# Float32 exponentials of the score tiles written back into their PSUM bank

## The chip, the cores and the metric

The kernel runs on one core of one Trainium2 chip. The metric is the device time of one execution in microseconds (us); lower is better. Engines are named as the profile names them: PE (TensorE, with PEld for its weight loads), DVE (VectorE), ACT (ScalarE), POOL (GpSimd) and SP (SyncE, which here issues most DMAs).

## What is computed

Three layers follow each other: causal attention with a decay bias (4 batches, 8 heads, 576 positions, head size 64), a mixture of 8 experts that gives each token to one expert, and a gated layer with a convolution of three taps. The change lies in the attention:

```
scores = scale * np.matmul(q, k.transpose(0, 1, 3, 2))
bias = -(cum[:, :, :, None] - cum[:, :, None, :])
scores = np.where(causal, -1000000000.0, scores + np.minimum(bias, 0.0))
scores = scores - np.max(scores, axis=-1, keepdims=True)
attn = np.exp(scores)
attn = attn / (np.sum(attn, axis=-1, keepdims=True) + 1e-09)
return np.matmul(attn, v).astype(np.float32)
```

## The kernel before

The attention works in 8 units of 4 heads each (two units to a batch). Matrix products run on float16 numbers in pairs: a float32 number is held as a high float16 part and a low one, the difference between the number and its high part.

A unit has 14 score tiles. A head has three tiles of 128 x 512 (`g` = 0, 1, 2), and every second head a fourth one of 128 x 64 columns (`g` = 3) for the last 64 positions of two heads. The program is one list of 112 steps, one score tile to a step, in a software pipeline that is written out by hand. In step t the loop at the end of `attention` issues, in this order:

- `rowmax` (L334, DVE): the row maxima of the piece of the step before, read from a PSUM tile `za`;
- `scores` of tile t (L438 and L441, PE): the products of `q` and `k` into a PSUM tile `z`;
- `piece` for a later unit (L331, PE): scores of the next unit into a PSUM tile `za`, from which its row maxima come, 14 pieces to a unit;
- `weights` of tile t-1 (L475 and L476, ACT): the exponential of `z`, once to float16 (`phi`) and once to float32 (`p`);
- `rest` of tile t-2 (L487, DVE): the difference `plo` = `p` - `phi`, a float16 tile;
- `values` (L503, PE) four steps behind, once for each head: the products of `phi` and `plo` with the values into a PSUM tile `o`; then `norm` and `xout` (L541 to L549, DVE) five and six steps behind.

One tile of each unit (third head, `g` = 0) is of another kind: its exponential stays one float32 tile `p0` (L471), and it has no difference.

When the last piece of a unit has been reduced, `max_cols` (L394 and L397, DVE) scales the maxima, `max_turn` (L407, PE) turns them and a DMA puts them into the operand of that unit's scores. POOL takes the low parts of `q` and `k` (L246, L247) and of `v` (L297 to L303), and those of the normed output (L560), all from SBUF into SBUF.

What keeps the engines in step are the buffers. There are three PSUM tiles `z` (pool `zps`), so `scores` of tile t need the bank of tile t-3. There are two PSUM tiles `za` (pool `aps`), so a piece needs the reduction of the piece two before it. `p` has three SBUF tiles (pool `pp`, named p32), `phi` and `plo` have eleven each. Each engine runs its own instructions in the order of the program, and waits on semaphores of the others.

After the attention (from about 263 us) come the routing of the tokens, a chain of small DVE instructions, the splitting of expert weights into two parts (L1034 on DVE), and the two other layers, in which PE is nearly always busy.

Of the kernel before, what the change touches and what calls it, by code (L numbers as in the profile page):

```python
# [9 lines left out]
F32 = mybir.dt.float32  # L10
F16 = mybir.dt.float16
# [27 lines left out]
def bc(ap, shape):  # L39
    return ap.to_broadcast(shape)  # L40


class Keep:
# [6 lines left out]
PAR = {'u1': {'sv': -6, 'pa': -10, 'pn': 4, 'mx': -3},  # L50
 'u2': {'at': (-24, -23, -20, -20, -19, -16), 'lv': -15, 'sv': -2, 'pa': -14, 'pn': 8, 'mx': -6},
 'u3': {'load': -37, 'loadq': 6, 'at': (-33, -28, -28, -27, -24, -22), 'sv': -1, 'pa': -19, 'pn': 14, 'mx': -5},
 'u': {'load': -48,
       'loadq': 8,
       'at': (-38, -34, -28, -31, -23, -23),
       'lv': -8,
       'sv': -4,
       'pa': -20,
# [56 lines left out]
def attention(tc, ctx, q, k, v, s, xd, rt, hook):  # L115
# [10 lines left out]
    def pool(n, b, on=ctx, **kw):  # L126
        return on.enter_context(tc.tile_pool(name=n, bufs=b, **kw))

    const, vp, natv = pool("const", 1), pool("vv", 2), pool("natv", 1)
    pp, p0p, php, wk, xp, xtp = pool("p32", 3), pool("p0", PAR["h"]["p0"]), pool("phl", PAR["h"]["ph"]), pool("wk", 2), pool("xs", 2), pool("xt", 1)  # L130
    zps, aps, ops, mps = (pool(n, b, space=PSUM) for n, b in (("zps", 3), ("aps", 2), ("ops", 2), ("mps", 1)))
    dram = pool("exd", 1, space=bass.MemoryType.DRAM)
    ex, ext = dram.tile([3, 2, B * H, 256], F16, name="ex"), dram.tile([3, B * H, 64], F16, name="ext")
# [292 lines left out]
    def mode(x):  # L426

        return PAR["m"][3 * x[1] + x[2]] if x[2] < 3 else "a"
# [36 lines left out]
    def weights(x):  # L465

        n = 64 if x[2] == 3 else 512
        z = st[x]
        if mode(x) == "f":
            p = st[x] = p0p.tile([128, 512], F32, name="p0")  # L470
            A.activation(p, z, AF.Exp, bias=lnes, scale=1.0 / SC)  # L471
            return
        p, hi, lo = pp.tile([128, 512], F32, name="p"), php.tile([128, 512], F16, name="phi"), php.tile([128, 512], F16, name="plo")
        if mode(x) != "p":
            A.activation(hi[:, 0:n], z[:, 0:n], AF.Exp, bias=lnes, scale=1.0 / SC)  # L475
        A.activation(p[:, 0:n], z[:, 0:n], AF.Exp, bias=lnes, scale=1.0 / SC)  # L476
        st[x] = p, hi, lo
# [137 lines left out]
    def second_a():  # L615
# [12 lines left out]
        z=lambda: Q.dma_start(xd[NT:NT + 128].rearrange("p (j c) -> p j c", c=256), bc(zero[:, None], [128, 4, 256])))  # L628
# [32 lines left out]
    for t in range(N + 9):  # L661
# [13 lines left out]
        if at(1):  # L675
            weights(at(1))
# [669 lines left out]
def attn_moe_moe2(tc, q, k, v, s, wg, wl, w1, w2, w_in, conv, w_out, out):  # L1346
    nc = tc.nc
    w_in, conv, w_out = (t.bitcast(I32) for t in (w_in, conv, w_out))
    with tc.manual_schedule(), ExitStack() as ctx:
# [40 lines left out]

        rt = Routing(tc, keep)
        attention(tc, c3, q, k, v, s, xd, rt, hook)
        c3.close()
        with ExitStack() as c4:
# [62 lines left out]
```

## Time and profile before

| what | us |
|---|---|
| median of 3 runs | 747.02 |
| lowest and highest run | 743.34 and 748.52 |
| the profiled execution, whole | 745.7 |
| its span, from first to last instruction | 743.5 |
| PE busy, share of the span | 85% |
| DVE busy, share of the span | 62% |
| ACT busy, share of the span | 52% |
| POOL busy, share of the span | 36% |

The profile is of one execution. Busy time is the union of an engine's instructions; register, semaphore and DMA-issuing instructions are not counted. Consecutive instructions of an engine overlap a little, so the next one can start before the row's duration is over. A wait is put down to what ended it last. The attention's score tiles lie between about 37 and 263 us; the steps of units 2 to 6 lie between 117 and 245 us.

### The profile page before, as it was taken

Reading aid. Unit: us, or ns where it says so; the run is one execution under the profiler, and the core shown is the slowest. Engines: PE = TensorE matmul, PEld = TensorE weight load, DVE = VectorE, ACT = ScalarE, POOL = GpSimd, SP = SyncE. Lnnn points to the kernel's source line nnn. Section 1 sums busy time; section 2 is a strip of 40 time slices with the busy share of each in tenths; the row PEclk is TensorE's granted clock in tenths of the full one; section 3 lists DMA queues with packets and bytes.
Section 4 is the critical chain, followed back from the end, with each engine's and each line's share of the span. In section 5 each row is a group of like instructions: output and inputs, shape, how many; then the busy total and the mean of one; then the engine's idle time right before and its main releaser. Section 6 shows DMA issues by size and latency. Waiting matters only on the chain.

```text
span 743.5 us, 15702 instructions
## 1 busy us (share of the span) xinstructions
PE 631.6 (85%) x5301; PEld 387.1 (52%) x5301; DVE 464.3 (62%) x838; ACT 383.3 (52%) x640; POOL 265.3 (36%) x367
## 2 busy tenths in 40 slices
PE   0449669988988934779999999999879999999997
PEld 0226547766766832334444444444347776666443
DVE  5527558987979787962587759675108994465000
ACT  4135647666767875543464737352109975455110
POOL 9316757655645247922243443433200000000000
PEclk9999879888989975998999999999989999999999
DMA  9977697878768895399999999966256400000111
GB/s 182 200 138 140 158 165 145 136 165 180 128 142 220 248 265 191 86 220 300 237 281 316 240 295 186 255 146 135 68 97 112 65 1 29 29 15 28 58 43 56
DMA packets 197278, 113.37 MB, mean 152 GB/s; under 512 B 147286, under 2 KB 173182, under 8 KB 197182
## 3 DMA queue, kind: packets, MB, share of 16 engines
q1 hardware_dynamic: 192574, 99.14, 58.5%
q0 software_dynamic: 4272, 12.93, 6.1%
q8 instruction: 48, 0.79, 0.4%
q14 instruction: 48, 0.39, 0.2%
q10 hardware_dynamic: 336, 0.11, 0.1%
HBM read 62.20 MB, written 15.31 MB: 104 GB/s over the span
## 4 chain that ended last, share of the span: by engine, by line
PE 49%; DMA 6%; DVE 1%; issue 0%; ACT 0%; another core or an unknown queue 0%; ACTq 0%; SPq 0%; DVEq 0%
PE hp L1270 13%; PE o L1318 13%; PE hp L1078 12%; PE yp L1078 11%; DMA yd<-ys,idx 4%; DMA ht<-hs 2%; PE xp L1108 1%; DVE r L1034 1%; DMA yt<-yd 0%; DVE hs L1124 0%; ACT xt L1109 0%; DVE ys L1138 0%; ACT ys L1137 0%; ACT s L1321 0%
## 5 line engine op out<-in xcount | busy, mean ns | idle before, releaser
L1078 PE MATMUL hp<-r,xt 128*128 x504 | 114.9, 385 | 8.4 <-ACT xt L1109 5.9
L1078 PE MATMUL yp<-r,ht 128*128 x504 | 112.2, 379 | 1.7 <-PEq L1186 1.1
L1270 PE MATMUL hp<-yt,wi 128*128 128x288 f16 x768 | 97.1, 289 | 2.9 <-DMA yt<-yd 2.9
L334 DVE TENSOR_REDUCE mx<-za 128x1 f32<-128x512 f32 (+4 forms) x113 | 67.7, 612 | 50.1 <-PE za L331 49.6
L1318 PE MATMUL o<-wo,g 128*128 128x512 f16 x432 | 94.5, 379 | 0.0
L487 DVE TENSOR_TENSOR plo<-p,phi 128x512 f16<-128x512 f32 (+1 forms) x104 | 85.1, 819 | 6.4 <-ACT p L476 6.2
L1270 PEld LDWEIGHTS <-wi 128*128 128x128 f16 x768 | 75.8, 99 | 24.5 <-DMA yt<-yd 3.4
L1078 PEld LDWEIGHTS <-xt 128*128 128x128 f16 x504 | 49.9, 99 | 69.5 <-ACT xt L1109 9.1
L475 ACT ACTIVATE phi<-z,lnes 128x512 f16<-128x512 f32 (+1 forms) x104 | 65.5, 629 | 39.3 <-PE z L441 39.2
L1078 PEld LDWEIGHTS <-ht 128*128 128x128 f16 x504 | 48.5, 98 | 57.4 <-issue 1.8
L331 PE MATMUL za<-k 70*128 70x256 f16 (+2 forms) x160 | 40.4, 338 | 41.3 <-DMA k<-k 33.6
L1034 DVE SCALAR_TENSOR_TENSOR r<-st,r 128x512 f32 (+3 forms) x76 | 69.3, 980 | 8.1 <-ACT r L1023 4.7
L438 PE MATMUL z<-k 71*128 71x256 f16 (+2 forms) x320 | 60.5, 311 | 12.3 <-ACT phi L475 6.7
L1139 POOL DMA_INDIRECT yd<-ys,idx x21 | 21.6, 1028 | 135.6 <-DVEq L1062 84.3
L1318 PEld LDWEIGHTS <-g 128*128 128x128 f16 x432 | 42.3, 98 | 49.5
L476 ACT ACTIVATE p<-z,lnes 128x512 f32<-128x512 f32 (+1 forms) x104 | 65.6, 631 | 1.2 <-DVE plo L487 1.1
L1023 ACT ACTIVATE r<-st 128x512 f32 (+3 forms) x84 | 57.0, 760 | 15.4 <-SPq L1071 12.5
L503 PEld LDWEIGHTS <-phi 128*128 128x128 f16 (+2 forms) x896 | 53.4, 108 | 4.8 <-issue 1.0
L503 PE MATMUL o<-vv,phi 128*128 128x65 f16 (+1 forms) x832 | 54.3, 203 | 0.0
L438 PEld LDWEIGHTS <-k 71*128 71x128 f16 x576 | 39.7, 106 | 22.7 <-issue 10.9
L503 PE MATMUL o<-vv,plo 128*128 128x65 f16 (+1 forms) x416 | 51.2, 200 | 0.0
L1287 DVE SCALAR_TENSOR_TENSOR c<-hb,cw,c 128x576 f32<-128x576 f32 x32 | 26.1, 816 | 36.7 <-ACT c L1281 36.7
(255 smaller groups left out, 1018.6 us busy)
## 6 DMA issues: line engine op xcount, KB each, us to landing
st<-in_moe_w_dram SPq DMA_DIRECT2D x8, 2048.0 KB
st<-in_moe_w_dram SPq DMA_DIRECT2D x24, 512.0 KB
out_dram<-s SPq DMA_DIRECT2D x18, 256.0 KB
st<-in_k_dram SPq DMA_DIRECT2D x16, 256.0 KB
st<-in_q_dram SPq DMA_DIRECT2D x16, 256.0 KB
k<-k SPq DMA_DIRECT2D x16, 256.0 KB
xd<-xh SPq DMA_DIRECT2D x16, 256.0 KB
k<-in_moe_w_dram SPq DMA_DIRECT2D x8, 512.0 KB
```

Of the source, the lines that this page charges most:

```text
L331: PE.matmul(out, lhsT=l, rhs=r, start=start, stop=stop, skip_group_check=True)
L334: return lambda: V.tensor_reduce(out, z.rearrange("p (e c) -> p e c", e=m), axis=AX.X, op=ALU.max)
L438: PE.matmul(out, lhsT=ks[i], rhs=qs[i], start=first and not i, stop=False, skip_group_check=True)
L475: A.activation(hi[:, 0:n], z[:, 0:n], AF.Exp, bias=lnes, scale=1.0 / SC)
L476: A.activation(p[:, 0:n], z[:, 0:n], AF.Exp, bias=lnes, scale=1.0 / SC)
L487: (V if md == "a" else G).tensor_tensor(lo[:, 0:n], p[:, 0:n], hi[:, 0:n], op=ALU.subtract)
L503: PE.matmul(out, lhsT=w, rhs=x, start=first, stop=last, skip_group_check=True)
L1023: i = self.nc.scalar.activation(hi, src, AF.Copy, scale=self.scale[w])
L1034: i = nc.vector.scalar_tensor_tensor(lo, in0=src, scalar=sc, in1=hi, op0=ALU.mult, op1=ALU.subtract)
L1078: i = self.nc.tensor.matmul(out, lhsT=lhsT, rhs=self.rings[w][:, c, k, bass.ds(s, 1), f], **kw)
L1270: PE.matmul(st[x][:, n, 0:HN], lhsT=wi[:, c, k, m], rhs=t[:, n, a + k], start=k + a + c == 0, stop=k == 3 and a == 4)
L1318: PE.matmul(o, lhsT=g[:, a, k, 128 * i:128 * i + 128], rhs=wo[:, c, k], start=j == 0, stop=j == 23)
```

## The change

For the tiles with two parts, the float32 exponential (L476) no longer goes to an SBUF tile `p` but back into the PSUM tile `z` from which it is read, and the difference (L487) reads it there. The SBUF pool p32 with its three tiles goes.

```
-    pp, p0p, php, wk, xp, xtp = pool("p32", 3), pool("p0", PAR["h"]["p0"]), pool("phl", PAR["h"]["ph"]), pool("wk", 2), pool("xs", 2), pool("xt", 1)
+    p0p, php, wk, xp, xtp = pool("p0", PAR["h"]["p0"]), pool("phl", PAR["h"]["ph"]), pool("wk", 2), pool("xs", 2), pool("xt", 1)
...
-        p, hi, lo = pp.tile([128, 512], F32, name="p"), php.tile([128, 512], F16, name="phi"), php.tile([128, 512], F16, name="plo")
+        p, hi, lo = z, php.tile([128, 512], F16, name="phi"), php.tile([128, 512], F16, name="plo")
         if mode(x) != "p":
             A.activation(hi[:, 0:n], z[:, 0:n], AF.Exp, bias=lnes, scale=1.0 / SC)
         A.activation(p[:, 0:n], z[:, 0:n], AF.Exp, bias=lnes, scale=1.0 / SC)
```

No instruction changes its place on any engine. What changes are the waits. On PE, the first tile of unit 2 stands in the program of before as follows (`k12` and `k2` are operands of that unit's scores, `k10` that of the piece for unit 3; a name in brackets is the engine or DMA queue whose semaphore is waited for):

```order
L438 LDWEIGHTS k12_143 [waits DMAHW7_49,DMAHW6_49]
L438 MATMUL z_1511<-k12_143 128x512 [waits Activation_49]
L438 LDWEIGHTS k2_619
L438 MATMUL z_1511<-k2_619 128x512
L441 LDWEIGHTS identm_135
L441 MATMUL z_1511<-trik_137,identm_135 128x128
L331 LDWEIGHTS k10_141
L331 MATMUL za_1515<-k10_141 128x256 [waits DVE_49]
```

And the same place now:

```order
L438 LDWEIGHTS k12_140 [waits DMAHW7_49,DMAHW6_49]
L438 MATMUL z_1483<-k12_140 128x512 [waits DVE_49]
L438 LDWEIGHTS k2_609
L438 MATMUL z_1483<-k2_609 128x512
L441 LDWEIGHTS identm_132
L441 MATMUL z_1483<-trik_134,identm_132 128x128
L331 LDWEIGHTS k10_138
L331 MATMUL za_1487<-k10_138 128x256 [waits PE_49]
```

The scores' first matmul waited for ACT (the exponentials of the tile three steps before) and now waits for DVE (the difference of that tile). The piece behind it waited for DVE (the reduction of the piece two before); that reduction stands in DVE's order ahead of the difference, so the earlier wait covers it.

## Rows read from the trace of the kernel before

**Rows 1.** The page: span; busy us, share of span, instructions per engine.

```profile
span 743.5 us, 15702 instructions
...
PE 631.6 (85%) x5301; PEld 387.1 (52%) x5301; DVE 464.3 (62%) x838; ACT 383.3 (52%) x640; POOL 265.3 (36%) x367
```

**Rows 2.** The chain that ended last: first piece (start us, us, what).

```profile
310.48 0.09 issue
```

**Rows 3.** Stretches: us; busy PE, PEld, DVE, ACT, POOL; clock, DMA share, GB/s.

```profile
45.00:117.00 72.00, 51.65 (x605) 38.74 (x606) 41.97 (x83) 38.05 (x70) 45.21 (x83) 0.88 0.77 149
117.00:245.00 128.00, 111.47 (x1728) 89.57 (x1727) 110.76 (x238) 86.73 (x160) 72.13 (x87) 0.88 0.76 162
245.00:263.00 18.00, 17.55 (x373) 15.45 (x371) 14.84 (x44) 16.32 (x33) 2.31 (x2) 1.00 0.93 275
263.00:335.00 72.00, 43.08 (x310) 22.75 (x308) 57.96 (x94) 39.59 (x58) 44.86 (x40) 0.80 0.74 186
```

**Rows 4.** The same stretches, line L487 (difference) alone: DVE busy us (x count).

```profile
45.00:117.00 72.00, 18.68 (x23) 0.88 0.77 149
117.00:245.00 128.00, 56.29 (x66) 0.88 0.76 162
245.00:263.00 18.00, 10.11 (x15) 1.00 0.93 275
```

**Rows 5.** Waits, 117 to 245 us: who, what for: us, times, longest.

```profile
DVE mx L334 <- PE za L331: 10.4, 16, 1.6
...
PE mt L407 <- DVE m L397: 6.8, 4, 2.0
PE za L331 <- DVE mx L334: 6.5, 9, 1.8
```

**Rows 6.** Of single lines: ns min/median/max, first and last start us, forms.

```profile
L487 DVE TENSOR_TENSOR plo<-p,phi x104: 194/684/2100, 46.9 to 262.3; 128x512 f16<-128x512 f32 x88, 128x64 f16<-128x64 f32 x16
...
L1124 DVE SCALAR_TENSOR_TENSOR hs<-hp,hs x42: 675/682/692, 309.1 to 517.7; 128x512 f16<-128x512 f32 x42
...
L547 DVE TENSOR_TENSOR x<-o,rc x32: 410/418/425, 70.9 to 264.7; 128x256 f32<-128x256 f32 x32
...
L476 ACT ACTIVATE p<-z,lnes x104: 303/679/780, 46.2 to 261.4; 128x512 f32<-128x512 f32 x88, 128x64 f32<-128x64 f32 x16
...
L1123 ACT ACTIVATE hs<-hp x42: 571/597/597, 301.7 to 515.3; 128x512 f16<-128x512 f32 x42
```

**Rows 7.** Timeline of DVE (start us, us, engine, line, operation), 189 to 210 us.

```profile
189.80 2.10 DVE L487 TENSOR_TENSOR plo<-p,phi 128x512 f16<-128x512 f32 x1
...
192.29 1.05 DVE L487 TENSOR_TENSOR plo<-p,phi 128x512 f16<-128x512 f32 x1
...
193.99 0.80 DVE L487 TENSOR_TENSOR plo<-p,phi 128x512 f16<-128x512 f32 x1
...
195.70 1.57 DVE L487 TENSOR_TENSOR plo<-p,phi 128x512 f16<-128x512 f32 x1
...
197.66 0.68 DVE L487 TENSOR_TENSOR plo<-p,phi 128x512 f16<-128x512 f32 x1
...
199.12 1.07 DVE L487 TENSOR_TENSOR plo<-p,phi 128x64 f16<-128x64 f32 x1
...
209.90 0.18 DVE L397 TENSOR_SCALAR m<-mx 128x18 f16<-128x18 f32 x1
```

**Rows 8.** Timeline of POOL, from the same stretch.

```profile
189.23 2.12 POOL L247 TENSOR_TENSOR st<-st,st 128x1024 f16<-128x1024 f32 x1
...
194.33 2.39 POOL L302 TENSOR_TENSOR vv<-nv,vv 128x1024 f16<-128x1024 f32 x1
```

**Rows 9.** Timeline of PE, from the same stretch.

```profile
196.62 0.62 PE L438 MATMUL z<-k 71*128 71x128 f16 x6
...
203.88 0.63 PE L438 MATMUL z<-k 71*128 71x128 f16 x6
...
210.14 0.28 PE L407 MATMUL mt<-id,m 128*18 128x128 f16 x1 [1.74 <-DVE m L397]
```

## Prediction

> **What bounds the kernel now.** I read the page first, then the chain that ended last, then the stretches of the attention, the line that the change touches, the waits, and at last one stretch step by step. The page shows no engine that is full over the whole span [rows 1]; an average over stages says little here. The chain is followed back only to 310.48 us [rows 2]; behind that point PE runs almost without a gap, and none of it is touched. What the change can move is when the attention ends, and so when the 72 us of routing and weight splitting begin, in which DVE is busy for 57.96 us with work in a fixed order [rows 3]. I take it that a microsecond saved in the attention is a microsecond saved at the end.
>
> Within the attention the stretch from 117 to 245 us (units 2 to 6) counts. Of its 128 us PE is busy for 111.47 and DVE for 110.76, ACT for 86.73, POOL for 72.13 [rows 3]. So two engines are near full, and each waits for the other: DVE for the pieces of PE 10.4 us, PE for reductions 6.5 us and for the scaled maxima 6.8 us [rows 5]. Neither is the only bound. In 45 to 117 us no engine is full (PE 51.65, DVE 41.97, POOL 45.21 of 72), and from 245 to 263 us PE is (17.55 of 18), with ACT behind it at 16.32 [rows 3].
>
> **Part one: the difference becomes shorter.** The 104 differences take 194 to 2100 ns, with a median of 684 ns [rows 6]. The long ones lie beside POOL: the one at 189.80 us took 2.10 us while POOL's subtraction ran from 189.23 for 2.12 us, and the one at 195.70 took 1.57 us and ended at 197.27, after POOL's that ran from 194.33 to 196.72 had ended; one at 197.66 took 0.68 us [rows 7, 8]. Both the difference and POOL's subtraction read two operands in SBUF. DVE instructions with one operand in PSUM and one in SBUF show no such spread: 42 at L1124, of the same shape, took 675 to 692 ns, and 32 at L547, within the attention and so beside the same work of POOL, 410 to 425 ns [rows 6]. The changed difference is of this kind. I take 0.684 us for a full one and 0.2 us for a narrow one.
>
> In 117 to 245 us the differences are busy for 56.29 us in 66 instructions [rows 4]: a unit has 11 full and 2 narrow ones, which makes 56 full and 10 narrow here. At the short durations they need 56 x 0.684 + 10 x 0.2 = 40.3 us. DVE is freed of 16.0 us. In the same way 45 to 117 us frees 18.68 - (19 x 0.684 + 4 x 0.2) = 4.9 us, and 245 to 263 us 10.11 - (12 x 0.684 + 3 x 0.2) = 1.3 us. The bounds of a full difference from PSUM are the 0.68 of L1124 and, if POOL still held it up, today's mean, at which nothing is freed; by form I take the nearest row, L1124.
>
> [...]
>
> **Part two: the bank is held longer, and PE gets a new wait.** There are three banks. Until now scores of tile t waited for the exponentials of tile t-3, now for its difference. An example: scores began at 196.62 us [rows 9], and the difference of the tile three before ran from 197.66 to 198.34 [rows 7], so they would have come 1.72 us later. Behind the waiting matmul stand the piece of the same step and, every three or four steps, the values of a head; DVE waits for the piece, ACT for the scores. The wait for the reduction of the piece two before [rows 5] (6.5 us) falls, as it is covered by the new one. In short: PE could run ahead of DVE by about a step more than it can now.
>
> What this costs next to part one I worked out by going through 189.8 to 210 us by hand, each instruction at its duration in the timeline and behind what it waits for, with differences of 0.68 and 0.2 us. The five long differences there (2.10, 1.05, 0.80, 1.57 and a narrow one of 1.07 [rows 7]) free 1.42 + 0.37 + 0.12 + 0.89 + 0.87 = 3.7 us. What comes of it: DVE now overtakes PE three times and waits some 0.65 us each, for the values and pieces of a head (PE does not reach the scores behind a head's values before about 203.35, at 203.88 now [rows 9]); PE waits for differences twice, 0.3 and 0.5 us, in the short steps without values; and the scaled maxima at 209.90 [rows 7], on which PE waits for 1.74 us before 210.14 [rows 9], come at about 208.5, 1.4 us earlier. So 1.4 of 3.7 us reach the end, a share of 0.38, the new wait included. For 117 to 245 us this makes 0.38 x 16.0 = 6.1 us.
>
> **Part three: the rest.** The exponential that now writes PSUM has no row. The bounds: 0.597 us, the shortest row of an activation of this shape (L1123), and 0.780, the longest of L476; today's median is 0.679 [rows 6]. I take 0.679. Even 0.10 more on 56 tiles is 5.7 us of ACT, which has 128 - 86.73 = 41 us to spare there. The exponential's own wait for the freeing of `p` goes with the pool; three `z` banks take the place of three `p` tiles. From 245 to 263 us there are no pieces, and each set of scores will follow a difference: one difference of 0.7 us is lost once, not per tile, since ACT is behind PE there; against it stands part of the 1.3 us freed. I count both at nothing, with bounds of -0.5 and +0.7. From 45 to 117 us I also count nothing: with PE and DVE idle for 20 and 30 of 72 us, the engines wait on loads and on POOL; its bounds are 0 and 0.38 x 4.9 = 1.9 us gained.
>
> **The sum.** The profiled execution took 745.7 us, 2.2 more than its span and 1.3 below the median of 747.0. 745.7 - 6.1 = 739.6; put to the median, 740.9, told as 741.0.
>
> **The rivals.**
> First, the coupling wins. Its place is the head: after each head's values DVE has nothing left, as PE can no longer have a piece in store. In the walk that was three waits of 0.65 us over three heads; if it is two such waits at each of the 20 heads of units 2 to 6, 20 x 1.3 = 26 us are lost and 16.0 freed, and the time is 747.0 + 10 = 757. It decides from 0.8 us of lost DVE time per head (16.0 / 20). For it speaks that DVE already waits 10.4 us for pieces [rows 5]; against it that the long differences are what makes DVE late in the first place.
> Second, the gain stays off the path: DVE is freed, but PE at 111.47 of 128 us, its slower clock (0.88 there [rows 3]) and the loads set the pace, and the two effects cancel: 746.5, from 745 to 748. For it speaks that PE is as full as DVE.
> Third, most of it arrives: the 13.3 us in which PE waits for DVE 6.5 + 6.8, [rows 5] go, and the pace is PE's: 747.0 - 13.3 = 733.7. Against it stands the walk, in which two thirds are lost.
> That the change does not do what it says, so that differences stay long beside POOL, would leave only the new wait: 1.72 us of lead lost once or twice in each of five units, 8.6 to 17 us, 756 to 764. L547 speaks against it; I count it with the first rival.
>
> **How the numbers follow.** The forecast has a chance of 0.48, the first rival 0.20, the second 0.20, the third 0.12. About 1% (7.5 us) is what a measurement of this kernel can tell from no change. The forecast's own range is 736 to 745. The range of 8 in 10 leaves out the far half of the first rival and the low end of the third: 732 to 754. Faster by over 1% (below 739.5): four tenths of the forecast's range, 0.20, and the third rival, 0.12, with a little over for its bounds: 0.33. Slower by over 1%: the first rival, 0.20. Within 1%: 0.47.
>
> **What would show it.** Right: every full difference at 0.68 to 0.70 us, also beside POOL, and L487 at some 63 us in all; DVE busy in the attention 20 us less; scores waiting for differences often, under 0.6 us each; the last difference 5 to 8 us earlier. Wrong: differences over 1 us; float32 exponentials of over 0.8 us; DVE's waits for pieces grown from 10 us to over 25; or an attention that ends early while the chain of the routing ends no earlier.

## The result

The changed kernel took 737.29 us (median of 4 runs, 735.95 to 738.79) beside 747.4 us for the kernel before on the same chip: a ratio of 0.9882, with a 95% interval of 0.9841 to 0.9924. Forecast were 741.0 us and a range of 732 to 754. Two more measurements, each beside its own runs of the kernel before, gave 0.987 (0.9818 to 0.9921) and 0.9972 (0.993 to 1.0014). So the gain lies between 0.3% and 1.3%, and the last measurement by itself cannot be told from no gain; the sections below come back to that. (The medians given here are of all runs; the ratios leave disturbed runs out, so the two can differ by some tenths of a per cent.)

The page of the changed kernel: span, and busy us of each engine, as [rows 1].

```profile
span 736.3 us, 15742 instructions
...
PE 625.4 (85%) x5301; PEld 383.7 (52%) x5301; DVE 443.8 (60%) x838; ACT 380.8 (52%) x640; POOL 251.2 (34%) x367
```

DVE lost 20.5 us and POOL 14.1: the two had held each other up, and both got shorter. POOL's subtraction of 128 x 1024 at L302 took 2052 to 2441 ns in the kernel before, with a median of 2367, and takes 2056 to 2073 now, with one of 2062. PE lost 6.2 us too, with the same 5301 matmuls, and no edit made a matmul shorter. Over the whole span it was granted a clock of 0.950, beside 0.940 before. These 6.2 us cannot be credited to the change: in a second trace of each kernel (again_before and third_after, below) PE is busy for 625.5 us in the kernel before and for 631.7 in the changed one. The stretches of the changed kernel (columns as in [rows 3]):

```profile
45.00:117.00 72.00, 51.45 (x580) 38.58 (x580) 38.91 (x85) 37.52 (x70) 42.33 (x85) 0.86 0.77 149
117.00:245.00 128.00, 111.92 (x1817) 90.32 (x1816) 98.20 (x252) 89.21 (x168) 62.24 (x87) 0.93 0.81 168
245.00:263.00 18.00, 15.57 (x335) 13.74 (x332) 12.20 (x38) 13.57 (x27) 1.15 (x1) 1.00 0.97 288
```

In the 128 us of the middle row DVE is busy for 98.20 us instead of 110.76. PE is busy as long as before (111.92 beside 111.47), but with 1817 matmul records instead of 1728, at a granted clock of 0.93 instead of 0.88. In this pair of traces more of the attention fits into the same stretch. The second trace of the kernel before shows that this is not steady: there the stretch has more records still, at 0.89.

```profile
117.00:245.00 128.00, 114.66 (x1839) 93.15 (x1839) 113.03 (x255) 91.14 (x170) 74.24 (x90) 0.89 0.80 168
```

The difference alone, in the same stretches (as [rows 4]), and its line with minimum, median and maximum in ns, with that of the exponential that now writes PSUM (as [rows 6]):

```profile
45.00:117.00 72.00, 14.26 (x23) 0.86 0.77 149
117.00:245.00 128.00, 41.79 (x69) 0.93 0.81 168
245.00:263.00 18.00, 7.18 (x12) 1.00 0.97 288
```

```profile
L487 DVE TENSOR_TENSOR plo<-z,phi x104: 193/681/693, 47.3 to 259.4; 128x512 f16<-128x512 f32 x88, 128x64 f16<-128x64 f32 x16
...
L476 ACT ACTIVATE z<-z,lnes x104: 279/653/718, 46.6 to 258.6; 128x512 f32<-128x512 f32 x88, 128x64 f32<-128x64 f32 x16
```

The same work of POOL that held the differences up in [rows 7, 8] now runs beside short ones. POOL's timeline of the changed kernel:

```profile
187.10 2.13 POOL L247 TENSOR_TENSOR st<-st,st 128x1024 f16<-128x1024 f32 x1
...
191.66 2.06 POOL L302 TENSOR_TENSOR vv<-nv,vv 128x1024 f16<-128x1024 f32 x1
```

and DVE's:

```profile
188.11 0.68 DVE L487 TENSOR_TENSOR plo<-z,phi 128x512 f16<-128x512 f32 x1
...
191.93 0.68 DVE L487 TENSOR_TENSOR plo<-z,phi 128x512 f16<-128x512 f32 x1
...
206.40 0.19 DVE L397 TENSOR_SCALAR m<-mx 128x18 f16<-128x18 f32 x1
```

No difference is above 0.693 us, where 2.10 stood before; the median is where it was. The exponential, now written to PSUM, became 26 ns shorter at the median (679 to 653).

The waits in 117 to 245 us (who, for what: us, times, longest; as [rows 5]):

```profile
DVE mx L334 <- PE za L331: 15.8, 17, 3.6
...
PE z L438 <- DVE plo L487: 6.0, 15, 0.6
...
PE za L331 <- DMA k<-k: 4.2, 2, 2.8
PE mt L407 <- DVE m L397: 3.6, 5, 1.0
```

The wait of a piece for the reduction two before it (6.5 us) is no longer listed; the new wait of the scores for the difference, 6.0 us, stands in its place, never above 0.6. PE's wait for the scaled maxima fell from 6.8 us (longest 2.0) to 3.6 (longest 1.0), because DVE reaches them earlier. So PE's waits for DVE fell from 13.3 to 9.6 us.

One wait is new: 4.2 us for the transfer of `k` (L264), the operand of the next unit's pieces. In 117 to 245 us all five traces of the changed computation have it (4.2 to 6.8 us: this one, again_after, third_after and the two with unused tiles, below), and none of the four of kernels without the new wait and with POOL at work (before, again_before, nohold, four_before). A part of the lead is lost there. The head of a unit near 155 us shows it; first PE's turned maxima and the piece behind them, and the issue of the transfer by SP (SPq), in the kernel before:

```profile
158.04 0.28 PE L407 MATMUL mt<-id,m 128*18 128x128 f16 x1 [1.16 <-DVE m L397]
...
159.28 0.63 PE L331 MATMUL za<-k 70*128 70x128 f16 x4
...
154.21 1.38 SPq L264 DMA_DIRECT2D k<-k  x2
```

and in the changed kernel:

```profile
153.07 0.22 PE L407 MATMUL mt<-id,m 128*18 128x128 f16 x1 [0.40 <-DVE m L397]
...
157.23 0.38 PE L331 MATMUL za<-k 70*128 70x128 f16 x4 [2.83 <-DMA k<-k]
...
152.54 1.37 SPq L264 DMA_DIRECT2D k<-k  x2
```

The maxima are turned 5.0 us earlier, but the transfer is issued only 1.7 us earlier, PE waits 2.83 us for it, and the piece comes 2.05 us earlier. On average over the five traces and the two of the kernel before a lead of 6.1 us becomes one of 3.2 at this place. What sets the time of that issue, and what an earlier one would bring, was not tried.

The clock of the two traces parts at the head of unit 3. Three stretches of the kernel before around 132 us, same columns:

```profile
122.00:131.60 9.60, 7.87 (x141) 6.08 (x139) 9.37 (x20) 8.09 (x15) 7.03 (x5) 1.00 0.54 137
131.60:138.40 6.80, 6.43 (x62) 4.95 (x62) 5.85 (x12) 2.82 (x6) 6.55 (x10) 0.50 0.91 171
138.40:155.00 16.60, 14.78 (x268) 12.38 (x266) 15.63 (x38) 11.66 (x20) 7.36 (x8) 1.00 0.78 138
```

and of the changed kernel:

```profile
122.00:131.60 9.60, 8.82 (x153) 6.93 (x152) 8.13 (x21) 8.75 (x16) 6.41 (x6) 1.00 0.63 153
131.60:138.40 6.80, 5.90 (x110) 5.05 (x108) 5.14 (x12) 3.51 (x8) 6.55 (x11) 1.00 1.06 149
138.40:155.00 16.60, 14.27 (x242) 11.11 (x240) 15.31 (x46) 13.32 (x25) 6.67 (x8) 1.00 0.84 151
```

In the kernel before the clock is 0.50 for the 6.8 us of the middle stretch, and PE, though busy for 6.43 us, gets through 62 matmuls; in the changed kernel it is 1.00 and 110 are done in 5.90 us. (The counts are not of like things throughout: more of the short products of `values` fall into the changed kernel's stretch.) What PE did before the clock fell is in its timeline (start, us, ..., and in brackets what it waited for); before:

```profile
128.67 0.41 PE L331 MATMUL za<-k,t 70*64 70x512 f16 x2 [0.30 <-DVE mx L334]
...
131.70 0.59 PE L331 MATMUL za<-k 70*128 70x128 f16 x4 [1.41 <-DVE mx L334]
...
132.98 0.58 PE L331 MATMUL za<-k 70*128 70x256 f16 x2 [0.27 <-DVE mx L334]
...
135.31 0.28 PE L407 MATMUL mt<-id,m 128*18 128x128 f16 x1
```

and in the changed kernel:

```profile
126.88 0.26 PE L438 MATMUL z<-t 71*64 71x64 f16 x4 [0.57 <-DVE plo L487]
...
129.80 0.61 PE L438 MATMUL z<-k 71*128 71x128 f16 x6 [0.21 <-DVE plo L487]
...
130.70 0.39 PE L331 MATMUL za<-k 70*128 70x128 f16 x4
...
133.57 0.22 PE L407 MATMUL mt<-id,m 128*18 128x128 f16 x1 [0.90 <-DVE m L397]
```

Before, PE stood for 1.41 us in one go while DVE was late with a reduction, and the next matmuls took 0.59 us at a clock of 0.50, where the same ones in the changed kernel took 0.39 at 1.00. In the changed kernel the waits for DVE around that place are of 0.57, 0.21 and 0.90 us, and the clock stays. The two facts stand side by side; that the one makes the other is not shown. Elsewhere the clock of the changed kernel falls too: after the wait of 2.83 us above it is 0.50 from 157.70 to 160.90 us. The two kernels reach that point at much the same time; at the turned maxima the changed one is 1.74 us ahead (133.57 beside 135.31).

### The profile page after: what moved, and what is told of

It is laid out like the page before. It is cut to its first block, busy times and chain, and to the rows that moved or that the text cites. A ratio compares the mean times of both kernels' runs of the same rounds, so it can differ in the third digit from the quotient of the medians.

```text
span 736.3 us, 15742 instructions
## 1 busy us (share of the span) xinstructions
PE 625.4 (85%) x5301; PEld 383.7 (52%) x5301; DVE 443.8 (60%) x838; ACT 380.8 (52%) x640; POOL 251.2 (34%) x367
## 5 line engine op out<-in xcount | busy, mean ns | idle before, releaser
L1078 PE MATMUL hp<-r,xt 128*128 x504 | 112.2, 379 | 7.3 <-ACT xt L1109 7.3
L1270 PE MATMUL hp<-yt,wi 128*128 128x288 f16 x768 | 95.5, 286 | 2.8 <-DMA yt<-yd 2.8
L438 PE MATMUL z<-k 71*128 71x256 f16 (+2 forms) x320 | 58.6, 302 | 14.2 <-DMA k<-mr 11.0
L487 DVE TENSOR_TENSOR plo<-z,phi 128x512 f16<-128x512 f32 (+1 forms) x104 | 63.2, 609 | 9.4 <-ACT z L476 9.3
L476 ACT ACTIVATE z<-z,lnes 128x512 f32<-128x512 f32 (+1 forms) x104 | 62.8, 604 | 0.0
```

The costliest lines, as they stand in the source:

```text
L438: PE.matmul(out, lhsT=ks[i], rhs=qs[i], start=first and not i, stop=False, skip_group_check=True)
L487: (V if md == "a" else G).tensor_tensor(lo[:, 0:n], p[:, 0:n], hi[:, 0:n], op=ALU.subtract)
L1078: i = self.nc.tensor.matmul(out, lhsT=lhsT, rhs=self.rings[w][:, c, k, bass.ds(s, 1), f], **kw)
L1270: PE.matmul(st[x][:, n, 0:HN], lhsT=wi[:, c, k, m], rhs=t[:, n, a + k], start=k + a + c == 0, stop=k == 3 and a == 4)
```

## The experiments

Three sets, each on one chip with its own runs of the kernel before. The clock is that of each kernel's one trace.

| set, kernel | median us (runs) | ratio to before, 95% interval | clock, 117 to 245 us |
|---|---|---|---|
| first measurement: before | 747.4 (4) | | 0.88 |
| changed | 737.29 (4) | 0.9882 (0.9841 to 0.9924) | 0.93 |
| one: before | 746.43 (23) | | |
| again_after | 737.63 (6) | 0.987 (0.9818 to 0.9921) | 0.92 |
| hold | 753.98 (6) | 1.0102 (1.0054 to 1.015) | 0.84 |
| nohold | 748.31 (12) | 0.9973 (0.9929 to 1.0017) | 0.89 |
| first_after | 739.78 (12) | 0.9907 (0.987 to 0.9944) | 0.85 |
| two: before | 746.14 (35) | | |
| again_before | 742.53 (10) | 0.9959 (0.9916 to 1.0001) | 0.89 |
| quiet_before | 741.3 (12) | 0.9944 (0.9907 to 0.9982) | 0.89 |
| quiet_after | 739.6 (12) | 0.994 (0.9908 to 0.9973) | 0.92 |
| pad_after | 741.04 (12) | 0.9942 (0.9911 to 0.9973) | 0.93 |
| three: before | 745.0 (35) | | |
| third_after | 741.39 (12) | 0.9972 (0.993 to 1.0014) | 0.91 |
| pad_after2 | 741.46 (12) | 0.999 (0.9954 to 1.0026) | 0.93 |
| four_after | 741.37 (12) | 0.9941 (0.9894 to 0.9988) | 0.88 |
| four_before | 748.46 (12) | 1.0065 (1.0023 to 1.0107) | 0.88 |

**Both kernels again (again_after, again_before, third_after), unedited.**

> The changed kernel once more, for an interval of its own and a second trace. Every theory expects a ratio to the kernel before of 0.985 to 0.992 (736 to 741 us beside 747). In the first pair of traces the last difference of the attention came only 2.9 us earlier and the end 7.2 us earlier; the other 4.3 us arose after the attention, where PE had half its clock at other times. If these 4.3 us are chance, the time behind the attention differs here from that of the first trace by some microseconds; if they belong to the change, it is as short as there.

> The kernel before once more, for a second trace. Every theory expects a ratio of 1.00. If the transfer of the transposed hidden rows in the second layer, 11 us in the first trace, and the half clock after it belong to the kernel, they are there again; if they are chance, the stretch from the routing table to the first output of the second layer may be 4 us shorter here.

> The changed kernel once more, beside three of its variants on one chip. Theory (the gain is the end of the long differences, about 9 us of 747): ratio to the kernel before 0.985 to 0.991, 736 to 740 us. Rival (the first two measurements were favoured by their chips, and half of the gain is scatter): ratio 0.992 to 0.997. The differences stay at 0.68 to 0.69 us either way.

The changed kernel repeated the first result on one chip and came to 0.9972 on another, against the 0.985 to 0.991 that I had expected there. That is the end of the range named for the rival (0.992 to 0.997), by which the first two measurements were favoured and half of the gain is scatter. The kernel before, run as if it were another kernel, came out at 0.9959 of itself: with 10 to 35 runs a difference below about half a per cent says little. So the size stands only roughly: 0.3% to 1.3%, by measurement.

**The new wait alone (hold, nohold).** The kernel before, its exponentials still in SBUF, with the difference as an instruction that does the same arithmetic (the first step is a bypass) and names a column it does not use: in hold a column of the score tile's bank, so that the scores of tile t wait for the difference of tile t-3; in nohold one in SBUF. The edit of hold:

```
-        st[x] = p, hi, lo
+        st[x] = p, hi, lo, z
...
-        p, hi, lo = st[x]
+        p, hi, lo, z = st[x]
...
-        (V if md == "a" else G).tensor_tensor(lo[:, 0:n], p[:, 0:n], hi[:, 0:n], op=ALU.subtract)
+        V.scalar_tensor_tensor(lo[:, 0:n], in0=p[:, 0:n], scalar=z[:, 0:1], in1=hi[:, 0:n], op0=ALU.bypass, op1=ALU.subtract)
```

and of nohold:

```
-        (V if md == "a" else G).tensor_tensor(lo[:, 0:n], p[:, 0:n], hi[:, 0:n], op=ALU.subtract)
+        V.scalar_tensor_tensor(lo[:, 0:n], in0=p[:, 0:n], scalar=lnes, in1=hi[:, 0:n], op0=ALU.bypass, op1=ALU.subtract)
```

> The new wait alone. The float32 exponential goes to SBUF as before; the difference reads a column of the PSUM tile as a pointer that it does not use, so that scores wait for the difference as in the changed kernel, and the difference still has two operands in SBUF. To be compared with the kernel called nohold, in which that pointer is a column in SBUF. Theory A (the gain is the end of the blocking beside POOL, the wait costs little): hold is 2 to 6 us slower than nohold, and slower than the kernel before. Rival B (the wait costs nothing or helps): within 1 us of nohold. Rival C (coupling is dear, and hidden in the change by a larger gain): over 8 us slower than nohold.

> The comparison for hold: the same form of the difference with an unused pointer in SBUF. The pointer makes a difference some 0.065 us longer, by the rows of L1138 against L1124. All theories: 1 to 5 us slower than the kernel before (104 x 0.065 = 6.8 us of DVE, under half of it on the path).

The difference in hold, then in nohold, and in hold the wait of the scores for it, 117 to 245 us:

```profile
L487 DVE SCALAR_TENSOR_TENSOR plo<-p,z,phi x104: 258/749/2606, 47.2 to 272.6; 128x512 f16<-128x512 f32 x88, 128x64 f16<-128x64 f32 x16
```

```profile
L487 DVE SCALAR_TENSOR_TENSOR plo<-p,lnes,phi x104: 254/744/2681, 47.4 to 264.7; 128x512 f16<-128x512 f32 x88, 128x64 f16<-128x64 f32 x16
```

```profile
PE z L438 <- DVE plo L487: 13.0, 18, 1.4
```

The differences are much alike in the two kernels, so it is the wait that sets them apart. With the differences still long, it is 13.0 us, up to 1.4 at a time, where the changed kernel has 6.0 and 0.6. It makes the kernel slower: 1.0102 against 0.9973, whose intervals do not touch. The clock in that stretch is 0.84, beside 0.89 in nohold. So the wait has a price of about 1.3% (1.0102 / 0.9973), some 9.6 us, or 5 to 14 with both intervals, as long as the differences are long. That is more than the 2 to 6 us of theory A; it is what rival C named, a coupling that is dear and hidden in the change by a larger gain. The change pays for its wait by making the differences short.

nohold came out otherwise than every theory had it: not 1 to 5 us slower than the kernel before but at 0.9973 of it, at most 0.2% slower by its interval, though its pointer makes the difference 744 ns at the median instead of 684. More DVE time alone did not show in the time.

**POOL without its subtractions (quiet_before, quiet_after).** In both kernels the low parts that POOL takes in the attention (of `q`, `k`, `v` and the normed output) are left out, with the scaling ahead of them, and set to zero; the rest stands.

```
-            G.tensor_scalar(a, a, scale[n], 0.0, op0=ALU.mult, op1=ALU.add)
-            G.tensor_tensor(h[:, :, i], a, h[:, :, 1 - i], op=ALU.subtract)
+            G.memset(h[:, :, i], 0.0)
...
-                G.tensor_scalar(x, x, VS, 0.0, op0=ALU.mult, op1=ALU.add)
-                G.tensor_tensor(dl, x, dh, op=ALU.subtract)
+                G.memset(dl, 0.0)
...
-        eng.tensor_tensor(xh[:, :, 1], x, xh[:, :, 0], op=ALU.subtract)
+        if eng is G:
+            G.memset(xh[:, :, 1], 0.0)
...
```

> The kernel before without POOL's subtractions of the attention: the low parts of q and k (units 2 to 7), of v (units 1 to 7) and of the normed output (units 0 to 6) are not computed but set to zero, which writes SBUF and reads none of it. Theory A (the long differences are blocked by POOL's reads): every full difference takes 0.66 to 0.72 us, as in the changed kernel, though both operands lie in SBUF; the attention ends 6 to 14 us earlier than before. Rival (the length has another cause, as the form of the operands): differences of over 1 us remain.

> The changed kernel with the same work of POOL left out and set to zero. Beside quiet_before only the new wait and the exponential's write into PSUM are left of the change. Theory A: no gain any more; equal to quiet_before or 1 to 6 us slower, from the new wait. Rival (a good part of the gain is the shorter exponential or the missing wait on a p tile): 3 us or more faster than quiet_before.

The cause of most of the long differences is shown. In the trace of the kernel before 31 differences are above 0.75 us, and 27 of them overlap a subtraction of POOL's; in that of quiet_before it is 7, and none does. In the changed kernel 42 differences overlap such a subtraction, and none is above 0.693 us.

Of the time the pair says less. Without the subtractions the two kernels are alike, 0.9944 and 0.994: that fits a gain that is the end of the contention, with a new wait and a shorter exponential that cost or bring nothing that can be measured. But the two intervals leave room for a difference of some 3 us either way, where the changed computation gains 4 us on that chip (pad_after, below), and again_before stood at 0.9959 there. Nor did the attention of quiet_before end 6 to 14 us earlier: its last difference begins at 256.8 us, beside 262.3 and 258.5 in the two traces of the kernel before.

The seven also mean that not every difference became short, as theory A had it. The longest that is left in the two traces looked at first like a contention that the change does not remove; DVE's timeline of quiet_after around it shows another cause:

```profile
132.59 3.06 DVE L395 TENSOR_SCALAR m<-mx 128x18 f16<-128x18 f32 x1
132.84 2.81 DVE L332 TENSOR_REDUCE mx<-za 128x2 f32<-128x512 f32 x1
133.44 2.21 DVE L485 TENSOR_TENSOR plo<-z,phi 128x512 f16<-128x512 f32 x1
```

and POOL's, at that time:

```profile
132.83 0.53 POOL L559 MEMSET xh<- 128x512 f16 x1
133.29 0.96 POOL L246 MEMSET h<- 128x1024 f16 x1
134.19 0.53 POOL L559 MEMSET xh<- 128x512 f16 x1
134.65 0.96 POOL L246 MEMSET h<- 128x1024 f16 x1
```

It is the scaled maxima (L395 here), 0.18 us in [rows 7], that take 3.06 us beside a row of memsets; the reduction and the difference stand behind them in DVE's order, and all three end at the same moment (135.65), just after the last memset (135.61).

**The place of later tiles in SBUF (pad_after, pad_after2).** The changed kernel keeps three unused tiles where the float32 exponentials lay.

```
-    p0p, php, wk, xp, xtp = pool("p0", PAR["h"]["p0"]), pool("phl", PAR["h"]["ph"]), pool("wk", 2), pool("xs", 2), pool("xt", 1)
+    pp, p0p, php, wk, xp, xtp = pool("p32", 3), pool("p0", PAR["h"]["p0"]), pool("phl", PAR["h"]["ph"]), pool("wk", 2), pool("xs", 2), pool("xt", 1)
...
+    for _ in range(3):
+        nc.gpsimd.memset(pp.tile([128, 512], F32, name="p")[:, 0:1], 0.0)
```

> The changed kernel with the pool p32 kept but not used (a column of each of its tiles is set once at the start), so that every other tile lies in SBUF where it lay in the kernel before. In all traces so far of kernels without that pool the stretch from the routing table to the first output of the second layer was 4 to 6 us shorter than in the kernel before. If the places in SBUF make it (transfers that meet each other there), the stretch is as long as in the kernel before, 48 to 50 us, and the ratio some 0.993; if they have no part in it, it stays at 43 to 45 us, and the ratio at 0.986 to 0.990.

> The changed kernel with the unused buffers of the float32 exponentials kept in SBUF, so that every later tile lies where it lies in the kernel before. Theory (the place of the tiles does not matter): within 0.3% of the changed kernel on this chip, and the attention ends within 2 us of its. Rival (part of the gain comes from where the later tiles lie in SBUF once the pool is gone): 0.5% to 0.7% slower than the changed kernel, as the earlier run of it stood (0.994 beside 0.988 on other chips), with the loss in the stretch behind the attention.

pad_after's ratio, 0.9942, is near the 0.993 that was named for the case that the places make the stretch behind the attention longer. That stretch does not follow the pool, though. From the routing table (`tab`) to the first output of the second layer (`ys`) it is 41.6 us in pad_after and 43.1 in pad_after2, 41.3 and 43.4 in the first and third trace of the changed kernel, and 43.4 and 41.3 in the two of the kernel before. On the third chip pad_after2 stands at 741.46 us beside 741.39 for the changed kernel, and the intervals overlap over most of their length: the place does not matter by more than can be measured. This also gives two more measurements of the same computation, 0.9942 and 0.999.

**Taking the new wait away (first_after, four_after, four_before).** first_after issues, in each step of the changed kernel, the difference on DVE ahead of the reduction. four_after gives the score tiles a fourth bank and puts the turned maxima into the two banks of the pieces; four_before does that to the kernel before.

```
+        at = lambda d: steps[t - d] if 0 <= t - d < N else None
+        if at(2):
+            rest(at(2))
...
-        if at(2):
-            rest(at(2))
```

```
-    zps, aps, ops, mps = (pool(n, b, space=PSUM) for n, b in (("zps", 3), ("aps", 2), ("ops", 2), ("mps", 1)))
+    zps, aps, ops = (pool(n, b, space=PSUM) for n, b in (("zps", 4), ("aps", 2), ("ops", 2)))
...
-        t = U[u, "mt"] = mps.tile([128, 512], F32, name="mt")
+        t = U[u, "mt"] = aps.tile([128, 512], F32, name="za")
```

> The changed kernel with one order changed on DVE: in each step the difference stands ahead of the reduction of the pieces, so that the bank is given back some 0.6 us earlier and the piece's bank as much later. If PE's waits for differences (9.4 us in the changed kernel's trace) lie on the path, it is 2 to 6 us faster than the changed kernel; if PE then waits for reductions instead, it is within 2 us of it or slower.

> The changed kernel with a fourth bank for the score tiles, taken from the tile of the unit maxima, which now shares the two banks of the reductions. The scores of tile t then wait for the difference of tile t-4. Theory (the wait for the bank still costs what the trace shows, 9.4 us of TensorE in the attention, of which a third to a half is on the path): the 7.6 us of waits of the z matmuls for the difference fall under 1 us, and the time is 2 to 4 us below the changed kernel's. Rival (TensorE waits for the reductions instead, as when the difference was put ahead of them): the waits for the difference go, those for mx<-za grow by as much, and the time is within 2 us of the changed kernel's or above it.

> The kernel before with the same fourth bank, to tell what the bank brings without the change. Theory (its scores wait for the exponentials only, for under 1 us in all, so a fourth bank has nothing to take away; the long differences stay at up to 2.1 us): within 2 us of the kernel before, 744 to 749 us. Rival (the shared bank of the unit maxima holds up the reductions): 2 to 6 us slower than before.

Neither can be told from the changed kernel: 0.9907 on a chip where it had 0.987, and 0.9941 where it had 0.9972, with intervals that overlap. first_after is as its second case had it (within 2 us or slower); the 2 to 4 us that theory named for four_after are neither shown nor excluded. The waits of the scores are indeed gone; in four_after, 117 to 245 us, PE waits for the maxima instead:

```profile
PE za L407 <- DVE m L397: 6.9, 5, 1.9
```

That is the 6.8 us, longest 2.0, of the kernel before [rows 5], where the changed kernel has 3.6. In first_after PE waits as long as 1.9 us for DVE at the same place. And both show the clock that the table has beside them: 0.85 and 0.88, with the fall near 132 us that the changed kernel does not have. A bank more for the kernel before costs it 0.65%, as the rival had it: its pieces now share their banks, and in 117 to 245 us PE waits 3.9 us for reductions ahead of the router's products (L838), which had shared a bank with the turned maxima alone.

**The clock, over all traces.** This reading came after the last run and has no experiment of its own; it rests on the traces of all runs. In the five traces of kernels that compute as the changed one does (the first, again_after, third_after and the two with unused tiles) the clock in 117 to 245 us is at half for 17.1 to 23.9 us, and none falls near 132 us. In the four of kernels without the new wait and with POOL at work (before, again_before, nohold, four_before) it is 27.3 to 30.7 us, each with that fall, between 123 and 136. The clock of that stretch does not settle how far a kernel gets in it: again_before has more matmul records there at 0.89 than the changed kernel at 0.93, and ends its attention earlier than four of the five. Over all runs that the ratios use, the mean granted clock of the whole span is 0.949 in 46 runs of the five (mean time 740.3 us) and 0.940 in 89 of the kernel before (744.5 us). Among the 89 runs of one and the same kernel a clock higher by 0.01 goes with 2.0 us less (fitted line). By that line the 0.0095 between the kernels goes with some 1.9 of the 4.2 us between the means. That is a correlation: no run sets the clock by itself, and that the change raises the clock, or that the clock brings these microseconds, is not shown. quiet_before gains 0.56% at a mean clock of 0.940, that of the kernel before.

## Why the prediction was right

**Part one** held to the last per cent. The difference is 0.681 us at the median from PSUM (0.684 taken, and 0.684 from SBUF in the kernel before), at most 0.693 beside POOL, and L487 needs 63.2 us in all (63 named). The row that it was taken from was weaker than it reads: of the 32 instructions at L547 only 5 overlap a subtraction of POOL's in the trace of the kernel before; the 42 differences of the changed kernel that do are the proof. In 117 to 245 us one costs 0.606 us (41.79 / 69) instead of 0.853 (56.29 / 66): 66 x 0.247 = 16.3 us of DVE freed, 16.0 forecast.

**Part two**, the new wait: many short ones (15 of at most 0.6 us, 0.3 and 0.5 in the walk), the wait for reductions swallowed, and DVE's wait for pieces up from 10.4 to 15.8 us, not to the 25 that would have meant the first rival. The case without the first part, differences that stay long and the wait alone, was put at 8.6 to 17 us; hold, beside nohold, measures some 9.6. The share was the weak spot. The walk had the scaled maxima near 209.9 us 1.4 us earlier; they came at 206.40, 3.5 us earlier in that trace, and 2.4 us earlier on average (five traces against the two of the kernel before, 207.9 and 210.3). The maxima before them were earlier still: at 150.8 to 153.8 us in five traces, at 157.8 to 161.2 in the four of kernels without the change. But the lead shrinks on the way: over the five and the two traces the turned maxima are 6.1 us earlier near 155 us, 3.0 near 185, 2.4 near 208 and 1.4 near 234. The walk lost its two thirds to three waits of DVE and two of PE for differences; in the traces PE also waits for the transfer of `k`, which comes little earlier, 4.2 to 6.8 us in 117 to 245 us. The second rival had named the loads. The walk had no load in it and kept every matmul at its duration of before. That a share of 0.38 came near the measured gain is in part luck.

**Part three**: the exponential was 0.653, not 0.679 us, within its bounds, and without weight, as forecast. The end of the attention did not come 5 to 8 us earlier: the last difference began at 259.40 us beside 262.26 in the two first traces, 2.9 us, and over five and two traces at 259.7 and 260.4. Single traces scatter here by 4 us (262.26 and 258.48 for the kernel before), more than the change brings. So this sign of being right did not come, and the traces do not show at which point of the program the gain of the runs arises.

**A microsecond saved in the attention is one at the end**: this could not be shown. Of the 7.2 us between the first two spans 4.3 arose after the attention (7.2 - 2.9), where nothing was changed. Most of it lies near 333 us, where the kernel before has the clock at half for 6.8 us after PE had waited 3.34 us for ACT, and ACT 2.51 us for the transfer of `ht`. That stretch is in the traces of before, nohold and third_after, and not in those of again_before, again_after and both with unused tiles: it comes and goes with neither kernel.

**The sum.** 6.0 us (747.0 - 741.0) were forecast. By the ratios 8.8 us were measured first (0.9882), then 9.7 (0.987) and 2.1 (0.9972), and 4.2 lie between the means over all chips. The forecast is inside that spread, which is too wide to prove the share of 0.38. The first two measurements lie in "faster by over 1%", to which a third was given, the third one within 1%, to which a half was. The third rival (733.7) came nearest in its reason, since PE's waits for reductions and maxima did shrink, from 13.3 to 3.6 us, but 6.0 came back as the wait for the difference and 4.2 as that for the transfer of `k`.

## What to carry to other kernels

Here a VectorE difference of two SBUF operands took up to 2.10 us beside a subtraction of GpSimd's, three times its median of 0.684; with one operand in PSUM, and the order untouched, it took at most 0.693 beside the same work. The buffer that is then held longer is a new wait: 13.0 us from 117 to 245 us in hold, where differences took up to 2.61 us, and 6.0 in the changed kernel, where none took over 0.693. Weigh the two together. Where TensorE alternates with another engine, ask of each wait that goes where the engine will stand next: here the waits for reductions (6.5 us) came back as waits for the difference (6.0 us) and for a transfer that was issued hardly earlier (4.2 us), and moving the new wait elsewhere brought nothing that could be measured. Read the granted clock by stretch, and take a second trace of each kernel before a difference in it is credited to a change.

## What the runs showed that was not expected

- The clock's part in it: in 117 to 245 us 0.91 to 0.93 in the traces of the changed computation, 0.88 and 0.89 in those of before, with PE busy for 110.4 to 112.6 us in the ones and 111.5 and 114.7 in the others. What makes it is open.
- Two orders that remove PE's new wait nearly wholly (to 0.4 us over the whole span in four_after) are not measurably faster; in four_after the wait for the maxima grew back to 6.9 us. Why the clock falls near 132 us in them too is not settled.
- An operation on 128 x 18 elements that takes 0.18 us took 3.06 us beside a row of POOL's memsets, in quiet_after, and 2.45 at the same place in quiet_before. In quiet_after it ended at 135.65 us, 0.04 after the last of them. What makes it long is not shown, and whether another engine for those memsets would free the maxima was not tried.
- The gain differs by measurement (0.987 to 0.997), and the kernel before is 0.4% from itself on one chip. Where two measurements of one pair stand apart by more than their intervals, only further chips tell the size.
